# Keys and queries in two 40-row transfers, gates in the value rows, fillers ahead of the states, gate sums in two parts

## The chip, the cores and the metric

The program runs on 1 core of one Trainium2 chip. The metric is the device time of one execution in microseconds (us). Before the change three runs took 391.96 us in the median (391.62 to 394.35).

## What is computed

The reference is an mLSTM layer (4 sequences, 8 heads, 768 steps, head size 40) whose rows go through a mixture of 16 experts (4 groups of 4, one expert for each of 3,072 rows):

```
for t in range(S):
    m_new = max(f_gate[t] + m, i_gate[t])
    f_stab, i_stab = exp(f_gate[t] + m - m_new), exp(i_gate[t] - m_new)
    C = f_stab * C + i_stab * outer(v[t], k[t]);  n = f_stab * n + i_stab * k[t]
    y[t] = sigmoid(o_gate[t]) * (C @ q[t]) / max(abs(n @ q[t]), 1)
x = y as 3072 rows of 320
g, e = best group, best expert in it (argmax of two softmaxes)
out = weight_g * weight_e * (relu(x @ w1[g, e]) @ w2[g, e])
```

## The kernel before, in words

The first 138 us or so are the attention, cut into 24 units: unit u is chunk c = u // 4 (128 steps) of sequence b = u % 4, all 8 heads. Then come the experts, with weights from HBM.

A unit's work is written by `unit(u)` (L780 to 831), and each engine takes its instructions in that written order. `loads(u + 3)` (L161) issues on SP's queue the keys and queries of three units ahead (`qk`, one transfer of 112 rows of 4 KB, of which rows 40 to 63 and 104 to 111 are zeros), then the rows of values and keys (`nt`, 128 rows). The output gates of a whole chunk come in one further transfer (`sig`, L153), and `gate_o` (L158) puts them through Tanh on ACT once a chunk. On PE `scores` (L179, tile sp) multiplies keys by queries; DVE masks the result (`masked`, tile pt); `state` (L196, tile Cp) adds the unit to the running states; `carried` (L213, from chunk 1 on) and `values` (L221, tile av) give the numerators and denominators; ACT copies the states to Cz (`state2`). The next unit finishes the rows of this one: `norm` and `rows` on DVE (den, xn; `rows` reads the gates), `rows2` on POOL (x), `turn` transposes x on PE (tile tp). `vscale(u + 1)` (L170) on POOL scales the next unit's values by their gate factors (tile vz, from nt) and stands ahead of `rows2(u - 1)` on that engine.

The gate factors come from `gate_sums(lo, hi)` (L837): two scans and some sums on DVE, transposes on PE, exponentials on ACT. It is a generator; `sum_on` takes its next step once a unit (L807). Chunk 0 is done ahead of unit 0, chunk 1 in units 0 to 2, chunks 2 to 5 in one piece of 512 columns in units 3 to 7; in unit 7 it ends with a test (over) that PE sums. `route` steps (router and slots of a row) are taken by `go_on`, as many in a unit as the tables MID and END say. `busy(n)` (L122) issues n matmuls of 512 columns whose result nobody reads: 11 at the start, 6 in unit 0 between `state` and `carried`.

At most eight transfers issued by SP and ACT are in flight: each waits for the one issued eight before it.

Of the kernel before, what the change touches and what calls it, by code (L numbers as in the profile page):

```python
# [7 lines left out]
F32 = mybir.dt.float32  # L8
# [3 lines left out]
AF = mybir.ActivationFunctionType  # L12
# [6 lines left out]
P = 128  # L19
# [15 lines left out]
NQK = 4  # L35
QR = 112
C_ID, C_UP, C_LT, C_TIE, C_E, C_P, C_CAP, C_FIRST, C_15E, C_BASE, C_IOTA, C_END = 0, 128, 256, 384, 388, 404, 405, 421, 437, 453, 469, 581
NV = 4
RANGE = 30.0
SEQ = 4 * D + 3  # L40

# [18 lines left out]


@with_exitstack
def lstm_moe(ctx: ExitStack, tc: tile.TileContext, gates, qkT, nat, og, wcat, w1, w2, cst, seq, out):
    nc = tc.nc
    enter = ctx.enter_context
    mm = nc.tensor.matmul
# [40 lines left out]

    ap_ = att_pool("att", 1)

    qkp = [ap_.tile([P, 2, 4, P], F32, name=f"qk{i}") for i in range(NQK)]  # L110
    vz = [ap_.tile([P, H, P], F32, name=f"vz{i}") for i in range(3)]
    Cz = ap_.tile([P, B * 4, P], F32, name="Cz")
    eb = ap_.tile([P, NCH, B * H], F32, name="eb")
# [31 lines left out]
    def load_qk(u):  # L145
        c, b = divmod(u, B)
        qk = qkp[u % NQK]
        nc.sync.dma_start(qk[0:QR], qkT[c, b])
        st_.setdefault(u, {})["qk"] = qk

    sigs = {}

    def load_o(c):  # L153
        t = wk.tile([P, B, DM], F32, name="sig")
        nc.sync.dma_start(t, og[:, c * B:(c + 1) * B, :])
        sigs[c] = t

    def gate_o(c):  # L158
        nc.scalar.activation(sigs[c], sigs[c], AF.Tanh, scale=0.5)

    def loads(u):  # L161
        c, b = divmod(u, B)
        if u > 1:
            load_qk(u)
        nt = natp.tile([P, 2 * DM], F32, name="nt")
        nc.sync.dma_start(nt, nat[c, b])
        st_[u]["nt"] = nt

# [68 lines left out]
    def rows(u):  # L237
        c, b = divmod(u, B)
        xn = st_[u]["xn"] = wk.tile([P, H, D], F32, name="xn")
        nc.vector.scalar_tensor_tensor(xn, sigs[c][:, b, :].rearrange("p (h d) -> p h d", d=D), 1.0, st_[u]["av"][:, :, 0:D],  # L240
                                       op0=ALU.add, op1=ALU.mult)

    def rows2(u):
# [522 lines left out]
    def run(stage, u):  # L766
        if 0 <= u < NU:
            stage(u)

    def do(tasks, n=99):  # L770
        while tasks and n:
            tasks.pop(0)()
            n -= 1
# [5 lines left out]

    def unit(u):  # L780
        run(loads, u + 3)
        if u == 6:
            first_tokens()
        if u % B == 1 and u // B + 1 < NCH:
            load_o(u // B + 1)
        run(scores, u)
        run(norm, u - 1)
        run(rows, u - 1)
        if u < NU - 2:
            run(vscale, u + 1)  # L790
        if u == NU - 3:
            run(vscale, u + 2)
        run(rows2, u - 1)
        run(lambda v: masked(v, 0), u)
        run(lambda v: masked(v, 1), u)
        do(lows)
        run(state, u)
        if u % B == 1 and 1 < u < EUNITS:
            logits_of(u - 5, u - 1)
        if u == EUNITS + 1:  # L800
            logits_of(EUNITS - 2, EUNITS)
        if u == NU - 1:
            logits_of(EUNITS, NU - 2)
        if u == 0:
            busy(6)
        if u < 8:
            sum_on(SUMS.get(u, 1))  # L807
        run(carried, u)
        run(turn, u - 1)
        do(backs)  # L810
        if u == 10:
            go_on(2)
            chores.insert(0, first_experts())
        if u == EUNITS + 3:
            chores.append(early_counts())
        go_on(MID.get(u, 0))
        if u == NU - 1:
            do(rt["turns"])
        run(values, u)
        run(state2, u)  # L820
        go_on(END.get(u, 0))
        if u == 3:
            first_entries()
        if u == 5:
            first_rows()
        if u % B == 3 and u // B + 1 < NCH:
            gate_o(u // B + 1)
        for _ in range(min(rt.get("old", 0), 1 if u < 16 else 2)):
            put_id()
        rt["old"] = len(ids)  # L830
# [5 lines left out]
    def gate_sums(lo, hi):  # L836
        fg, ig = G[:, 0, lo:hi], G[:, 1, lo:hi]  # L837
        q = nc.gpsimd if lo == 0 else nc.vector
        init = NEG if lo == 0 else M_[:, lo - 1:lo]
        nc.vector.tensor_tensor_scan(M_[:, lo:hi], fg, ig, init, op0=ALU.add, op1=ALU.max)  # L840
        l1 = max(lo, 1)
        q.tensor_tensor(Cg[:, lo:hi], ig, M_[:, lo:hi], op=ALU.subtract)
        yield
        nc.vector.tensor_tensor(Dl[:, l1:hi], G[:, 0, l1:hi], M_[:, l1 - 1:hi - 1], op=ALU.add)
        nc.vector.tensor_tensor(Dl[:, l1:hi], Dl[:, l1:hi], M_[:, l1:hi], op=ALU.subtract)
        yield
        nc.vector.tensor_tensor_scan(A_[:, lo:hi], Dl[:, lo:hi], low[:, lo:hi], 0.0 if lo == 0 else A_[:, lo - 1:lo],
                                     op0=ALU.add, op1=ALU.max)
        q.tensor_tensor(Cg[:, lo:hi], Cg[:, lo:hi], A_[:, lo:hi], op=ALU.subtract)
        yield  # L850
        cl, ch = lo // P, hi // P
        tp = ps_1.tile([P, 512], F32, name="tp", tag="tp")
        n = ch - cl
        for i in range(n):
            s = slice((cl + i) * P, (cl + i + 1) * P)
            nc.tensor.transpose(out=tp[:, 32 * i:32 * i + 32], in_=Cg[:, s], identity=ident[0:32, 0:32])
            nc.tensor.transpose(out=tp[:, 32 * (n + i):32 * (n + i) + 32], in_=A_[:, s], identity=ident[0:32, 0:32])
        nc.scalar.activation(eb[:, cl:ch, :].rearrange("p c h -> p (c h)"), tp[:, 0:32 * n], AF.Exp)
        fl = floor[:, cl:ch, :].rearrange("p c h -> p (c h)")
        nc.scalar.activation(fl, tp[:, 32 * n:64 * n], AF.Exp, scale=-1.0)  # L860
        nc.vector.tensor_scalar(fl, fl, 2.0, None, op0=ALU.mult)
        if hi == S:
            yield
            over = post.tile([P, 1], BF16, name="over")[0:B * H]
            nc.vector.tensor_scalar(over, A_[:, S - 1:S], -RANGE, None, op0=ALU.is_le)
            tp = ps_1.tile([P, 512], F32, name="tp", tag="tp")
            mm(tp[:, 0:1], ones_b[0:B * H], over, start=True, stop=True)
            nc.vector.tensor_scalar(wide, tp[:, 0:1], 1.0, None, op0=ALU.min)
# [8 lines left out]
    with tc.manual_schedule():  # L877
        nc.sync.dma_start(G[:, :, 0:P], gates[:, :, 0:P])
        nc.scalar.dma_start(cs[:, 0:C_LT], cst[:, 0:C_LT])
        nc.scalar.dma_start(G[:, :, P:], gates[:, :, P:])  # L880
        nc.scalar.dma_start(cs[:, C_LT:], cst[:, C_LT:])
        nc.vector.memset(ones_b, 1.0)
        nc.vector.memset(ones16, float(NE))
        nc.vector.memset(sep, 0.0)
        nc.scalar.activation(sep, sep, AF.Exp)
        busy(11)
        nc.vector.memset(low, -RANGE)
        nc.vector.memset(Dl[:, 0:1], 0.0)
        nc.vector.memset(ohsum[0], 0.0)
        for t in Cp:  # L890
            nc.vector.memset(t, 0.0)
        for t in vz:
            nc.gpsimd.memset(t, 0.0)
        nc.gpsimd.memset(Cz, 0.0)
        load_qk(0)
        loads(0)
        load_qk(1)
        loads(1)
        load_o(0)
        loads(2)  # L900
        sums.append(gate_sums(0, P))
        sum_on(9)
        vscale(0)
        gate_o(0)
        nc.vector.tensor_copy(keyb, cs[:, C_15E:C_15E + NE])
        nc.vector.tensor_copy(lt_b, cs[:, C_LT:C_LT + P])
        nc.vector.tensor_copy(base_b, cs[:, C_BASE:C_BASE + NE])
        nc.sync.dma_start(wc, wcat)
        sums.append(gate_sums(P, 2 * P))
        sums.append(gate_sums(2 * P, S))  # L910
        for u in range(0, 5):
            unit(u)
    pools["ws"] = [wsa]
# [269 lines left out]
def _lay(inputs):  # L1183
# [5 lines left out]

    def tr(a):  # L1190
        a = a.reshape(B, H // 2, 2, NCH, P, D).transpose(3, 0, 2, 5, 1, 4)
        a = np.concatenate([a, np.zeros_like(a[:, :, :, :64 - D])], axis=3)
        return a.reshape(NCH, B, P, H // 2, P)[:, :, 0:QR]

    qkT = c(np.stack([tr(k), tr(q)], axis=3))

    def rows(a):
        return a.reshape(B, H, NCH, P, D).transpose(2, 0, 3, 1, 4)

    nat = c(np.concatenate([rows(v).reshape(NCH, B, P, DM), rows(k).reshape(NCH, B, P, DM)], axis=-1))  # L1200
    og = c(rows(o).reshape(NCH * B, P, DM).transpose(1, 0, 2))
    wg, we = inputs['moe_w_group'], inputs['moe_w_expert']
    wcat = np.concatenate([wg, we.transpose(1, 0, 2).reshape(DM, NE)], axis=1)
    wcat = np.pad(wcat, ((0, 0), (0, 12)))
# [21 lines left out]

    one = np.ones((S, B * H, 1), v.dtype)
    seq = c(np.concatenate([steps(q), steps(k), steps(v), one, steps(o), steps(inputs['f_gate']), steps(inputs['i_gate'])], axis=-1))
    return {'gates': gates, 'qkT': qkT, 'nat': nat, 'og': og, 'wcat': wcat, 'w1': w1, 'w2': w2, 'cst': cst, 'seq': seq}


# [20 lines left out]
```

## Time and profile before

| | us |
|---|---|
| median of three runs | 391.96 |
| the profiled execution, its own time | 389.81 |
| its span, first to last instruction | 387.9 |
| PE busy | 368.6 (95%) |
| DVE / ACT / POOL busy | 242.6 / 176.9 / 141.1 |

The profile follows one execution. Its chain of waits goes back from the last instruction, at each step to what released it. PE's busy share is not its share at its peak, since PE also runs at a lower granted clock in places. A stage is read by the wait that ends last in it.

### The profile page before, as it was taken

The page shows a single profiled execution, that of the slowest core. Times are in us where ns is not written, and L with a number is a line of the kernel's source. Part 1 is how long each engine was busy: PE and PEld are TensorE (multiplying, and loading weights), DVE is VectorE, ACT ScalarE, POOL GpSimd, SP SyncE. Part 2 cuts the span into 40 slices and gives each one's busy share as a digit, 9 for nine tenths or more (in the row PEclk, how much of TensorE's full clock was granted, in tenths as well). Part 3 has the DMA queues.
Part 4 walks back from the last instruction along what each step waited for, and adds up shares of the span by engine and source line. Part 5 has one row for each costly group of instructions (what it writes and reads, how often), then busy time and mean ns, then how long its engine had stood idle before and what let it go on. Part 6 is the DMA issues. An engine that isn't in the chain of part 4 may idle for free.

```text
span 387.9 us, 8856 instructions
## 1 busy us (share of the span) xinstructions
PE 368.6 (95%) x3313; PEld 348.1 (90%) x3313; DVE 242.6 (63%) x629; ACT 176.9 (46%) x411; POOL 141.1 (36%) x201
## 2 busy tenths in 40 slices
PE   6999999999998998899999999999999999999993
PEld 2688889989887998889999999999999999999993
DVE  4378757768777678466797757675574824554510
ACT  2233343426342233456665647656466633554520
POOL 6245225544646224625224253413413323233110
PEclk9799999999999899969999999999999999999998
DMA  7998767699983900859149977659525487669500
GB/s 190 304 323 265 199 192 234 182 325 289 318 276 92 356 32 1 246 172 356 69 129 414 373 268 259 198 183 355 179 84 182 165 306 251 226 254 328 189 19 16
DMA packets 26996, 85.34 MB, mean 220 GB/s; under 512 B 8800, under 2 KB 12339, under 8 KB 23362
## 3 DMA queue, kind: packets, MB, share of 16 engines
q1 hardware_dynamic: 18562, 66.35, 51.1%
q0 software_dynamic: 4560, 13.16, 10.1%
q10 hardware_dynamic: 3824, 5.18, 4.0%
q8 instruction: 28, 0.46, 0.5%
q14 instruction: 22, 0.18, 0.2%
HBM read 75.85 MB, written 9.10 MB: 219 GB/s over the span
## 4 chain that ended last, share of the span: by engine, by line
PE 80%; DVE 6%; issue 6%; DMA 4%; POOL 1%; POOLq 1%; ACT 1%; SPq 0%; DVEq 0%
PE psh L701 14%; PE av L225 10%; PE psh L669 8%; PE po L724 7%; PE po L725 7%; PE po L723 7%; PE sp L185 6%; PE av L218 4%; DMA nt<-in_nat_dram 4%; PE po L729 2%; PE tpm L251 2%; PE po L728 2%; PE tp L251 2%; PE Cp L202 2%; DVE pt L190 1%
## 5 line engine op out<-in xcount | busy, mean ns | idle before, releaser
L532 POOL DMA_INDIRECT out_dram<-y,ix x32 | 38.2, 1193 | 72.4 <-ACT y L735 57.9
L723 PE MATMUL po<-w2h,hh 128*128 128x320 f32 (+3 forms) x200 | 63.6, 318 | 0.0
L724 PE MATMUL po<-w2l,hh 128*128 128x320 f32 (+3 forms) x200 | 62.4, 312 | 0.0
L725 PE MATMUL po<-w2h,hh 128*128 128x320 f32 (+3 forms) x200 | 62.3, 311 | 0.0
L528 POOL DMA_INDIRECT xg<-x_d,ix x32 | 32.9, 1029 | 74.0 <-DMA ix<-itab 44.5
L596 DVE TENSOR_TENSOR w2l<-w2s,w2h 128x640 fp32r<-128x640 f32 x64 | 50.4, 817 | 12.7 <-ACT w2h L594 11.5
L225 PE MATMUL av<-vz,pt 128*128 128x128 f32 x384 | 49.8, 285 | 0.2
L658 DVE SCALAR_TENSOR_TENSOR hh<-psh,hh 128x240 fp32r<-128x240 f32 (+6 forms) x108 | 36.3, 366 | 21.1 <-ACT hh L655 20.1
L225 PEld LDWEIGHTS av<-vz,pt 128*128 128x128 f32 x384 | 47.2, 199 | 1.6 <-PE busy L128 1.0
L655 ACT ACTIVATE hh<-psh 128x288 fp32r<-128x288 f32 (+8 forms) x68 | 30.1, 443 | 32.9 <-PE psh L701 16.4
L594 ACT CAST w2h<-w2s 128x640 fp32r<-128x640 f32 x64 | 43.2, 722 | 0.0
L669 PE MATMUL psh<-xhl,w1s 128*128 128x144 f32 (+3 forms) x336 | 41.3, 283 | 0.0
L669 PEld LDWEIGHTS psh<-xhl,w1s 128*128 128x128 f32 x336 | 40.9, 191 | 0.0
L701 PE MATMUL psh<-xhl,w1h 128*128 128x256 f32 (+5 forms) x224 | 37.4, 289 | 0.0
L723 PEld LDWEIGHTS po<-w2h,hh 128*128 128x128 f32 (+3 forms) x200 | 36.6, 183 | 0.0
L724 PEld LDWEIGHTS po<-w2l,hh 128*128 128x128 f32 (+3 forms) x200 | 36.5, 183 | 0.0
L725 PEld LDWEIGHTS po<-w2h,hh 128*128 128x128 f32 (+3 forms) x200 | 36.5, 182 | 0.0
L735 ACT ACTIVATE y<-po,ix 128x320 f32<-128x320 f32 (+3 forms) x24 | 12.7, 529 | 48.3 <-PE po L725 41.6
L190 DVE TENSOR_TENSOR pt<-sp,cs 128x512 f32<-128x512 f32 x48 | 30.9, 685 | 3.3 <-PE sp L185 2.4
L433 POOL DMA_INDIRECT itab<-ent,slot x24 | 24.0, 1002 | 21.7 <-DVE ent L380 17.1
L701 PEld LDWEIGHTS psh<-xhl,w1h 128*128 128x128 f32 x224 | 31.2, 189 | 0.7 <-issue 0.2
L245 POOL TENSOR_TENSOR x<-xn,den 128x320 f32<-128x320 f32 x20 | 14.4, 722 | 43.7 <-DVE xn L240 29.6
(193 smaller groups left out, 683.6 us busy)
## 6 DMA issues: line engine op xcount, KB each, us to landing
w1s<-in_w_dram SPq DMA_DIRECT2D x13, 1536.0 KB
w2s<-in_w_dram SPq DMA_DIRECT2D x13, 1280.0 KB
qk<-in_qkT_dram SPq DMA_DIRECT2D x24, 448.0 KB
nt<-in_nat_dram SPq DMA_DIRECT2D x24, 320.0 KB
x_d<-x ACTq DMA_DIRECT2D x24, 192.0 KB
sig<-in_og_dram SPq DMA_DIRECT2D x6, 640.0 KB
w1s<-in_w_dram SPq DMA_DIRECT2D x8, 384.0 KB
w2s<-in_w_dram SPq DMA_DIRECT2D x8, 320.0 KB
```

The lines of the kernel that those rows point to most:

```text
L190: nc.vector.tensor_tensor(pt, t["pm"][r], bc(cs[:, C_UP:C_UP + P].unsqueeze(1), (P, 4, P)), op=ALU.mult)
L225: mm(t["av"][:, j * D1:j * D1 + P], t["pm"][j % 2][:, j // 2, :], t["vz"][:, j, :], start=(c == 0 and j == 0), stop=(j == H - 1), skip_gro ...
L528: return nc.gpsimd.indirect_dma_start(out=o, out_offset=None, in_=src, in_offset=bass.IndirectOffsetOnAxis(ap=idx, axis=0))
L532: return nc.gpsimd.indirect_dma_start(out=out, out_offset=bass.IndirectOffsetOnAxis(ap=idx, axis=0), in_=y, in_offset=None, bounds_check=N ...
L594: nc.scalar.copy(a, src[:, s])
L596: lows.append(lambda: nc.vector.tensor_tensor(o[rows], src[rows, s], a[rows].bitcast(F32), op=ALU.subtract))
L658: nc.vector.scalar_tensor_tensor(hh[:, f:f + per, dst], src[:, :, t], 0.0, hr.bitcast(F32)[:, :, t], op0=ALU.max, op1=ALU.subtract)
L669: ins = mm(ps[:, g * W:(g + 1) * W], w1s[:, s], xhl[:, k, :], start=(k == 0), stop=(k == 2))
L701: ins = mm(ps[:, g * W:(g + 1) * W], w[:, s], x, start=(n == 0), stop=(n == len(todo) - 1))
L723: mm(po[0:m], hh[:, f, t], w2h[:, s], start=st0, stop=False)
L724: mm(po[0:m], hh[:, f, t], w2l[:, s], start=False, stop=False)
L725: ins = mm(po[0:m], hh[:, f, tl], w2h[:, s], start=False, stop=sp0)
```

## The change

- Each unit's qk comes as two transfers of 40 rows (two pieces of 2 KB a row) straight into rows 0 to 39 and 64 to 103. The 32 zero rows are no longer sent; instead the query half of the four qk tiles is zeroed once, two tiles by DVE at the very start, two by POOL.
- The output gates are the last third of `nt` (128 rows of 3.75 KB instead of 2.5 KB), and the sig transfer goes. Tanh runs once a unit on 320 columns, after `values` and ahead of the Cz copies. There are five nt buffers instead of four.
- Fillers: 12 at the start instead of 11, 3 ahead of the first scores, and 5 between scores and state of unit 0 instead of 6 between state and values.
- POOL zeroes vz[2] and Cz after the first gate sums instead of ahead of them.
- The gate sums of chunks 2 to 5 come as 2 to 3 (units 3 to 6) and 4 to 5 (units 7 to 10), and the test over is made in unit 11 and summed on PE in unit 12.

```diff
-NV = 4
+NV = 5
...
-        nc.sync.dma_start(qk[0:QR], qkT[c, b])
-        st_.setdefault(u, {})["qk"] = qk
...
+        for r in range(2):
+            nc.sync.dma_start(qk[64 * r:64 * r + D], qkT[c, b, r].rearrange("g p t -> p g t"))
+        st_.setdefault(u, {})["qk"] = qk.rearrange("p g (h t) -> p g h t", t=P)
...
+    def gate_o(u):
+        o = st_[u]["nt"][:, 2 * DM:3 * DM]
+        nc.scalar.activation(o, o, AF.Tanh, scale=0.5)
...
-        nt = natp.tile([P, 2 * DM], F32, name="nt")
+        nt = natp.tile([P, 3 * DM], F32, name="nt")
...
-        if u % B == 1 and u // B + 1 < NCH:
-            load_o(u // B + 1)
...
         do(lows)
+        if u == 0:
+            busy(5)
         run(state, u)
...
-        if u == 0:
-            busy(6)
-        if u < 8:
+        if u < 13:
             sum_on(SUMS.get(u, 1))
...
         run(values, u)
+        gate_o(u)
         run(state2, u)
...
-        if u % B == 3 and u // B + 1 < NCH:
-            gate_o(u // B + 1)
...
             nc.vector.tensor_scalar(over, A_[:, S - 1:S], -RANGE, None, op0=ALU.is_le)
+            yield
...
+        for i in range(2):
+            nc.vector.memset(qkp[i][:, 1], 0.0)
...
-        busy(11)
+        busy(12)
...
-        for t in vz:
+        for t in (vz[0], vz[1], qkp[2][:, 1], qkp[3][:, 1]):
             nc.gpsimd.memset(t, 0.0)
-        nc.gpsimd.memset(Cz, 0.0)
...
-        load_o(0)
         loads(2)
         sums.append(gate_sums(0, P))
         sum_on(9)
+        busy(3)
+        nc.gpsimd.memset(vz[2], 0.0)
+        nc.gpsimd.memset(Cz, 0.0)
         vscale(0)
-        gate_o(0)
...
-        sums.append(gate_sums(2 * P, S))
+        sums.append(gate_sums(2 * P, 4 * P))
+        sums.append(gate_sums(4 * P, S))
```

PE at the start, before; tp are the gate sums, sp the scores, Cp the state, av the values of unit 0, and the last row is unit 1:

```order
L857 MATMUL tp<-cs,w2s 128x32
L185 MATMUL sp<-qk_100 128x128 x8
L202 MATMUL Cp_122<-vz_104,nt 40x41 x8
L128 LDWEIGHTS ones_b
L128 MATMUL busy<-ones_b 128x512
...
L225 MATMUL av_235<-vz_104,pt 128x128 x8
L185 MATMUL sp<-qk_101 128x128 x8
```

And now:

```order
L849 MATMUL tp<-cs,w2s 128x32
L128 LDWEIGHTS ones_b
L128 MATMUL busy<-ones_b 128x512
...
L180 MATMUL sp<-qk_100 128x128 x8
...
L197 MATMUL Cp_122<-vz_104,nt 40x41 x8
L220 MATMUL av_244<-vz_104,pt 128x128 x8
L180 MATMUL sp<-qk_101 128x128 x8
```

Nothing stands between state and values any more; three fillers stand ahead of the scores, five between scores and state.

POOL at the end of unit 3 and in units 4 and 5, before (the two vz are those of units 5 and 6, the two x those of units 3 and 4):

```order
L412 IOTA ent_74 128x2
L174 TENSOR_TENSOR vz_106<-nt,eb 128x8x40
L174 TENSOR_TENSOR vz_104<-nt,eb 128x8x40
L245 TENSOR_TENSOR x<-xn,den 128x320 x2
L418 MEMSET w1s 128x256
```

And now:

```order
L407 IOTA ent_74 128x2
L169 TENSOR_TENSOR vz_106<-nt,eb 128x8x40
L240 TENSOR_TENSOR x<-xn,den 128x320
L169 TENSOR_TENSOR vz_104<-nt,eb 128x8x40
L240 TENSOR_TENSOR x<-xn,den 128x320
```

The x of unit 3 no longer stands behind the vz of unit 6, which needs the nt of unit 6.

DVE in unit 7 behind the two masks, before:

```order
L190 TENSOR_TENSOR pt<-sp,cs 128x512 x2
L865 TENSOR_SCALAR over<-w2s 32x1
L868 TENSOR_SCALAR wide<-tp 128x1
L369 TENSOR_REDUCE sm<-ex 128x20
L371 TENSOR_SCALAR sm<-sm 128x20
```

And now:

```order
L185 TENSOR_TENSOR pt<-sp,cs 128x512 x2
L832 SCALAR_TENSOR_TENSOR w1s<-w1s 32x256
L834 TENSOR_TENSOR w1s<-w1s 32x256
L364 TENSOR_REDUCE sm<-ex 128x20
L366 TENSOR_SCALAR sm<-sm 128x20
```

The test over and its reader have left the unit; a scan and a subtraction of 256 columns have come.

## Rows read from the trace of the kernel before

**Rows 1.** The page's chain that ended last: shares of the span by engine

```profile
PE 80%; DVE 6%; issue 6%; DMA 4%; POOL 1%; POOLq 1%; ACT 1%; SPq 0%; DVEq 0%
```

**Rows 2.** Timeline of PE: start us, length us, instruction [idle before <-what ended it]

```profile
7.63 1.16 PE L185 MATMUL sp<-qk 40*128 40x128 f32 x16 [0.89 <-DMA qk<-in_qkT_dram]
10.04 0.78 PE L202 MATMUL Cp<-vz,nt 128*40 128x41 f32 x16 [1.25 <-POOL vz L174]
10.75 2.74 PE L128 MATMUL busy<-ones_b 128*128 128x512 bf16 x6
13.55 2.97 PE L225 MATMUL av<-vz,pt 128*128 128x128 f32 x16
16.45 1.16 PE L185 MATMUL sp<-qk 40*128 40x128 f32 x16
18.75 2.06 PE L225 MATMUL av<-vz,pt 128*128 128x128 f32 x16
20.75 1.16 PE L185 MATMUL sp<-qk 40*128 40x128 f32 x16
...
32.58 0.55 PE L251 MATMUL tp<-cs,x 128*128 128x128 f32 x3 [0.32 <-POOL x L245]
...
41.13 0.19 PE L328 MATMUL lg<-oh,lt_b 128*128 128x64 bf16 x1 [0.59 <-DVE oh L323]
...
49.31 0.17 PE L867 MATMUL tp<-over,ones_b 32*128 32x1 bf16 x1 [0.99 <-DVE over L865]
```

**Rows 3.** Timeline of POOL, units 0 to 2 and 4, columns as in Rows 2

```profile
9.27 0.72 POOL L174 TENSOR_TENSOR vz<-nt,eb 128x320 f32<-128x320 f32 x1 [2.89 <-DMA nt<-in_nat_dram]
...
16.39 0.72 POOL L174 TENSOR_TENSOR vz<-nt,eb 128x320 f32<-128x320 f32 x1 [4.07 <-DMA nt<-in_nat_dram]
17.59 0.72 POOL L245 TENSOR_TENSOR x<-xn,den 128x320 f32<-128x320 f32 x1 [0.48 <-DVE xn L240]
...
31.12 0.72 POOL L174 TENSOR_TENSOR vz<-nt,eb 128x320 f32<-128x320 f32 x1 [0.87 <-DMA nt<-in_nat_dram]
```

**Rows 4.** Busy time by stretch: length, engines' busy us, PEclk, DMA share, GB/s

```profile
5.75:8.84 3.09, 1.47 (x18) 1.17 (x18) 0.58 (x5) 0.50 (x3) 0.55 (x2) 0.97 1.06 285
8.84:15.25 6.41, 5.15 (x30) 3.06 (x31) 1.94 (x4) 1.67 (x4) 1.44 (x2) 0.50 1.04 309
...
122.00:124.00 2.00, 0.69 (x4) 0.49 (x5) 1.97 (x5) 0.38 (x2) 1.72 (x3) 1.00 0.02 1
124.00:128.00 4.00, 3.89 (x20) 3.48 (x22) 2.60 (x13) 0.35 (x1) 1.64 (x2) 0.59 0.82 238
```

**Rows 5.** The same for ten microseconds in the middle of the attention

```profile
80.00:90.00 10.00, 10.00 (x129) 9.19 (x125) 5.85 (x23) 4.16 (x13) 4.28 (x7) 1.00 1.04 318
```

**Rows 6.** The page's transfers by line: count, size of one

```profile
qk<-in_qkT_dram SPq DMA_DIRECT2D x24, 448.0 KB
nt<-in_nat_dram SPq DMA_DIRECT2D x24, 320.0 KB
...
sig<-in_og_dram SPq DMA_DIRECT2D x6, 640.0 KB
```

**Rows 7.** Chain of waits in order of time: start us, length us, what

```profile
22.42 8.57 DMA nt<-in_nat_dram
...
37.32 1.19 DVE w2s L847
38.53 1.03 DVE w1s L849
...
73.05 1.09 PE sp L185 x16
...
77.78 1.09 PE sp L185 x16
```

**Rows 8.** Groups by shape, first 60 us: busy us, mean ns | idle before

```profile
L159 ACT ACTIVATE sig<-sig 128x1280 f32<-128x1280 f32 x3 | 3.8, 1271 | 6.3 <-DMA sig<-in_og_dram 6.3
...
L891 DVE MEMSET Cp<- 128x512 f32 x2 | 1.0, 485 | 0.2
```

More of the change, by code (lines that the diff above doesn't have):

```diff
@@ L62, in lstm_moe @@
 @with_exitstack
-def lstm_moe(ctx: ExitStack, tc: tile.TileContext, gates, qkT, nat, og, wcat, w1, w2, cst, seq, out):
+def lstm_moe(ctx: ExitStack, tc: tile.TileContext, gates, qkT, nat, wcat, w1, w2, cst, seq, out):
     nc = tc.nc
@@ L108, in lstm_moe @@
     ap_ = att_pool("att", 1)
-    qkp = [ap_.tile([P, 2, 4, P], F32, name=f"qk{i}") for i in range(NQK)]
+    qkp = [ap_.tile([P, 2, 4 * P], F32, name=f"qk{i}") for i in range(NQK)]
     vz = [ap_.tile([P, H, P], F32, name=f"vz{i}") for i in range(3)]
@@ L147, in load_qk @@
         qk = qkp[u % NQK]
-        nc.sync.dma_start(qk[0:QR], qkT[c, b])
-        st_.setdefault(u, {})["qk"] = qk
[L151 to L159, printed above, removed]
+        for r in range(2):
[4 more added lines that the diff above has]
+        nc.scalar.activation(o, o, AF.Tanh, scale=0.5)
     def loads(u):
@@ L239, in rows @@
         xn = st_[u]["xn"] = wk.tile([P, H, D], F32, name="xn")
-        nc.vector.scalar_tensor_tensor(xn, sigs[c][:, b, :].rearrange("p (h d) -> p h d", d=D), 1.0, st_[u]["av"][:, :, 0:D],
+        nc.vector.scalar_tensor_tensor(xn, st_[u]["nt"][:, 2 * DM:3 * DM].rearrange("p (h d) -> p h d", d=D), 1.0, st_[u]["av"][:, :, 0:D],
                                        op0=ALU.add, op1=ALU.mult)
@@ L1191, in tr @@
         a = a.reshape(B, H // 2, 2, NCH, P, D).transpose(3, 0, 2, 5, 1, 4)
-        a = np.concatenate([a, np.zeros_like(a[:, :, :, :64 - D])], axis=3)
-        return a.reshape(NCH, B, P, H // 2, P)[:, :, 0:QR]
+        return a.reshape(NCH, B, 2, D, H // 2 * P)
     qkT = c(np.stack([tr(k), tr(q)], axis=3))
@@ L1198, in rows @@
         return a.reshape(B, H, NCH, P, D).transpose(2, 0, 3, 1, 4)
-    nat = c(np.concatenate([rows(v).reshape(NCH, B, P, DM), rows(k).reshape(NCH, B, P, DM)], axis=-1))
-    og = c(rows(o).reshape(NCH * B, P, DM).transpose(1, 0, 2))
+    nat = c(np.concatenate([rows(a).reshape(NCH, B, P, DM) for a in (v, k, o)], axis=-1))
     wg, we = inputs['moe_w_group'], inputs['moe_w_expert']
@@ L1228, in _lay @@
     seq = c(np.concatenate([steps(q), steps(k), steps(v), one, steps(o), steps(inputs['f_gate']), steps(inputs['i_gate'])], axis=-1))
-    return {'gates': gates, 'qkT': qkT, 'nat': nat, 'og': og, 'wcat': wcat, 'w1': w1, 'w2': w2, 'cst': cst, 'seq': seq}
+    return {'gates': gates, 'qkT': qkT, 'nat': nat, 'wcat': wcat, 'w1': w1, 'w2': w2, 'cst': cst, 'seq': seq}
 def kernel(**inputs):
```

## The prediction, made before the changed kernel was run

> **What bounds the kernel now.** I read the chain of waits first. PE carries 80% of it and transfers 4% [rows 1], so a microsecond counts only where it moves PE. In the middle of the attention one unit's scores start 4.73 us after the last unit's [rows 7] and PE is busy for all of a 10 us stretch [rows 5]: there PE alone sets the pace. Next I read PE's timeline for the places where it waits. The first 20 us are the slow part: unit 1's scores start only at 16.45 and unit 2's at 20.75 [rows 2]. Unit 0's values start at 13.55, although its state was there at 10.82; what stands between is 2.74 us of fillers [rows 2]. POOL's timeline shows the second limit: vz of unit 2 stood idle 4.07 us for its nt, started at 16.39, and x of unit 0 stands behind it, at 17.59 [rows 3]. The transfer engines were full all that time, share 1.04 at 309 GB/s [rows 4]. Later there are three short waits: 0.32 us for x of unit 3, 0.59 us for the router in unit 5, 0.99 us for the test over in unit 7 [rows 2].
>
> **Part 1, the start.** Without fillers behind the state, values of unit 0 can begin at 10.04 + 0.78 = 10.8. At unit 1's duration of 2.06 us they end near 12.9, so unit 1's scores come 3.5 us earlier than at 16.45 [rows 2]. That lead is not kept: unit 1 cannot turn unit 0's rows before x of unit 0, and x stands on POOL behind vz of unit 2, so nt of unit 2 decides. From vz to x is 0.72 us [rows 3], and from x to unit 2's scores 20.75 - 17.59 = 3.16 us [rows 2, 3]. Before, x also waited 0.48 us for xn [rows 3]; now xn is early, so even with nt landing when it does today 0.48 us is won.
>
> When does nt of unit 2 land? Ahead of its end the queue had three qk, three nt and one sig: 3 x 768 + 640 = 2,944 KB [rows 6]. Now it has 3 x (320 + 480) = 2,400 KB. At 309 GB/s the missing 544 KB are 1.8 us [rows 4]: the upper bound, a gain of 1.8 + 0.5 = 2.3 us. It holds if the sixteen transfer engines share a 40-row transfer evenly. All large loads so far have 112 or 128 rows, multiples of sixteen; 40 rows are not, and no row shows how they are dealt. If the busiest engine gets 3 of 40 rows of 4 KB, it carries 24 KB of keys and queries and 30 KB of nt a unit, 162 KB in three units, against 2,944 / 16 = 184 KB now: 22 KB less, 1.1 us at 309 / 16 = 19.3 KB/us. If it gets more, nt lands no earlier, or up to 1 us later (each unit's nt itself grows by 160 KB, 10 KB an engine, 0.5 us): the lower bound, a loss of about 0.5 us. I take 3 rows, the least a whole-row split allows: 1.1 + 0.5 = 1.6 us.
>
> The price is the clock. Unit 1's scores and state are done near 14.5 and PE then waits for x until about 16.5. After stretches in which PE was busy for 1.47 of 3.09 us, or 0.69 of 2.00, the granted clock was 0.50 in the next 6.41 us and 0.59 in 4 us [rows 4], the lower of its two levels, 1.2 GHz. Fillers bridge unit 0 now; none bridge unit 1. The bounds are nothing, if the clock stays, and 1.6 us, what the second of these stretches lost: 4 x (1 - 0.59). I take 0.9 us, the difference of unit 0's values at the lower clock and unit 1's at the higher, 2.97 - 2.06 [rows 2]. The start is then worth 1.6 - 0.9 = 0.7 us.
>
> The other moves at the start cost nothing. DVE's two memsets (2 x 0.485 us [rows 8]) delay the first scan by 1 us, but POOL's share of those sums no longer stands behind the memset of Cz, and the scores wait for qk until 7.63 anyway [rows 2]. POOL's vz[2] and Cz are zeroed while nt of unit 0 is under way (2.89 us of idling [rows 3]). If nt came earlier than that, the memsets would be late next. The first qk waits for one 0.485 us memset, behind SP's issue of the gates.
>
> **Part 2, x of unit 3.** On POOL it stood behind vz of unit 6, which waited until 31.12 for an nt that took 8.57 us [rows 3, 7]. It now stands ahead of it, and PE's 0.32 us [rows 2] go.
>
> **Part 3, gate sums.** In unit 5 DVE's scan of 512 columns and its subtraction, 1.19 + 1.03 us [rows 7], stand ahead of the router for which PE waits 0.59 us. With 256 columns each is shorter; if both halve, 1.1 us go, so all of the 0.59 goes. In unit 7 the 0.99 us for over go [rows 2]: over is made a unit ahead of its matmul. Against it stand about 1.1 us more of DVE work in each of units 7, 8 and 9, in units of 4.73 us, and four of the eight transposes move from unit 6 to unit 10. In unit 9 the new scan stands between the masks and the router. If that cover is gone, up to 0.6 us come back. I count none.
>
> **Part 4, Tanh.** Six of 1.27 us become 24 on a quarter of the columns, so at least 0.32 us each, and with a fixed share perhaps 0.5 [rows 8]. They stand ahead of the Cz copies, which are read four units later, and run beside `values`; the next unit's `rows` comes after `values`. Nothing, either way.
>
> **Sum.** 0.7 + 0.32 + 0.59 + 0.99 = 2.6 us. The profiled execution, 389.81 us with a span of 387.9, would come to 387.2. It was 2.15 us faster than the median of the runs, 391.96, and the forecast is for the median: **389.4 us**. What is won ahead of unit 8 shifts all that follows, since transfers, router and experts start relative to the units.
>
> **Rivals.**
> - **Everything is kept, 20%.** Forty rows are shared evenly and PE's clock stays up. The start is worth 2.3 us, the sum 4.2, the time 387.8. For it speaks that 14% fewer bytes go through full engines [rows 4, 6]; against it the idle time in unit 1.
> - **Ten engines carry the keys, 25%.** If a 40-row transfer is dealt over ten engines, four rows each, the busiest carry 320 / 10 + 480 / 16 = 62 KB a unit, against 928 / 16 = 58 KB now. Three units are 186 KB against 184: nt of unit 2 lands as late as before. The start wins 0.5 us and, with PE idle for some 3 us in unit 1, pays the clock's whole 1.6. With the other 1.9 us the sum is 0.8, the time 391.2. The Trainium skill says so ("DMA: Bandwidth & Descriptors", section "Why a DMA increments its semaphore by 16 and not by 1"): the engines used are the largest number up to 16 that divides the slowest dimension, as 100 partitions give 10. By that rule the time would be 391.2 rather than 389.4, and no run here shows it yet.
> - **The middle falls behind, 10%, slower.** From 80 us on the engines are full at 318 GB/s (share 1.04) while the first expert's weights load [rows 5]. With ten busy engines each unit takes 4 KB more on them, 0.2 us at 19.9 KB/us. Worse, SP has three loads a unit instead of 2.25, and only eight transfers may be in flight: with one weight load and one store a unit that is 8 / 5 = 1.6 units, 7.6 us, where landing took 8.57 [rows 7]. Ten such units lose 10 us of lead; the loads are issued three units, 14.2 us, ahead, so 14.2 - 8.57 = 5.6 us are spare. From the point where these are used up, PE waits for nt: some 4.4 us, less the 0.8 of the rival above, 395.6 us. Against it: today's chain has no such wait.
> - The remaining 45% are my forecast.
>
> **Range and chances.** About 1%, 3.9 us, is what a measurement of this kernel tells from no change. Faster by more needs nearly all of the first rival (below 388.0): 20% with the better end of the forecast. Slower by more (above 395.9) is half of the third: 6%. Within 1%: 74%. The range runs from 386.9, the first rival with both bounds of the small terms, to 393.0, the second rival with nt a microsecond late and the unit 9 cover gone.
>
> **What would show it.** Right: no fillers between Cp and av of unit 0, unit 1's scores near 13, vz of unit 2 near 15.3, unit 2's scores near 19 to 20, a stretch at half clock there; PE's waits for over and for the router in units 5 and 7 gone, none new in units 9 and 10. Wrong: vz of unit 2 at 16.4 or later (second rival), a granted clock of 1.00 throughout (first), or PE or POOL waiting for nt beyond 60 us (third).

## The result, and the profile after

The changed kernel took 388.5 us in the median of ten runs (385.58 to 391.75), the kernel before 392.15 in ten runs beside them: ratio 0.9889, 95% interval 0.9851 to 0.9926. A second series gave 388.55 us (twelve runs) against 391.38 (29 runs), ratio 0.9954, interval 0.9919 to 0.9988. The ratios leave out executions more than 1.5% above the shortest of their kernel, so they can differ from the ratio of the two medians. It is faster, by 2.8 to 3.7 us in the medians and 1.8 to 4.4 us by the ratios; forecast were 389.4 us and 2.6 us. The stages behind that sum came out otherwise than forecast.

The first profiled execution of the changed kernel was the longest of its ten, 391.75 us. Unless another is named, the rows below are of one near the median, 388.46 us, span 386.8. First PE's timeline of it, columns as in Rows 2:

```profile
7.71 1.16 PE L180 MATMUL sp<-qk 40*128 40x128 f32 x16
9.99 0.51 PE L197 MATMUL Cp<-vz,nt 128*40 128x41 f32 x16
10.52 2.33 PE L220 MATMUL av<-vz,pt 128*128 128x128 f32 x16
12.79 1.16 PE L180 MATMUL sp<-qk 40*128 40x128 f32 x16
13.88 0.51 PE L197 MATMUL Cp<-vz,nt 128*40 128x41 f32 x16
17.31 0.88 PE L246 MATMUL tp<-cs,x 128*128 128x128 f32 x3 [2.93 <-POOL x L240]
17.98 3.29 PE L220 MATMUL av<-vz,pt 128*128 128x128 f32 x16
21.20 1.16 PE L180 MATMUL sp<-qk 40*128 40x128 f32 x16
25.74 1.16 PE L180 MATMUL sp<-qk 40*128 40x128 f32 x16
...
32.56 0.49 PE L246 MATMUL tp<-cs,x 128*128 128x128 f32 x3
34.77 1.16 PE L180 MATMUL sp<-qk 40*128 40x128 f32 x16
...
40.37 0.19 PE L323 MATMUL lg<-oh,lt_b 128*128 128x64 bf16 x1
...
72.83 0.17 PE L860 MATMUL tp<-over,ones_b 32*128 32x1 bf16 x1
```

Against [rows 2]: unit 1's scores come 3.66 us earlier, at 12.79, but unit 2's, at 21.20, are 0.45 us later than at 20.75. Between them PE waits 2.93 us for x of unit 0. The waits for x of unit 3, for the router in unit 5 and for over are gone (32.56, 40.37 and 72.83 have no bracket). POOL's timeline shows why x is late:

```profile
12.40 0.72 POOL L169 TENSOR_TENSOR vz<-nt,eb 128x320 f32<-128x320 f32 x1 [2.66 <-DMA nt<-in_nat_dram]
15.74 0.72 POOL L169 TENSOR_TENSOR vz<-nt,eb 128x320 f32<-128x320 f32 x1 [2.61 <-DMA nt<-in_nat_dram]
16.42 0.84 POOL L240 TENSOR_TENSOR x<-xn,den 128x320 f32<-128x320 f32 x1
```

vz of unit 2 starts at 15.74, 0.65 us earlier than in [rows 3], and x of unit 0 stands behind it. Busy time by stretch, columns as in Rows 4:

```profile
14.00:15.00 1.00, 0.39 (x16) 0.26 (x14) 1.00 (x2) 0.00 (x0) 0.00 (x0) 1.00 0.74 271
15.00:16.00 1.00, 0.00 (x0) 0.00 (x0) 0.93 (x4) 0.00 (x0) 0.26 (x1) 1.00 0.70 220
...
16.00:18.00 2.00, 0.69 (x4) 0.69 (x5) 1.36 (x2) 0.24 (x1) 1.26 (x2) 0.84 0.89 247
18.00:20.00 2.00, 2.00 (x11) 2.00 (x11) 0.00 (x0) 1.53 (x5) 0.00 (x0) 0.50 0.86 311
20.00:22.00 2.00, 2.00 (x22) 1.88 (x23) 0.62 (x4) 0.00 (x0) 0.72 (x1) 0.81 0.84 266
```

While POOL waits for nt the transfer engines are busy for only 0.70 to 0.74 of the time (the number ahead of the last in a row), against 1.04 in [rows 4]. Behind the wait the granted clock falls to 0.50, the lower of its two levels. In the 391.75 us execution PE waited 3.52 us at that place and the clock then stayed at 0.50 until 30 us:

```profile
14.00:15.00 1.00, 0.00 (x0) 0.00 (x0) 1.00 (x3) 0.00 (x0) 0.00 (x0) 1.00 0.64 207
...
18.00:22.00 4.00, 4.00 (x20) 3.77 (x21) 0.14 (x1) 1.53 (x5) 0.72 (x1) 0.50 0.80 262
22.00:26.00 4.00, 3.53 (x37) 3.13 (x38) 2.24 (x7) 0.42 (x3) 1.47 (x2) 0.50 0.52 146
26.00:30.00 4.00, 4.00 (x22) 3.78 (x22) 0.22 (x2) 1.53 (x5) 0.00 (x1) 0.50 0.61 206
```

The page's transfers by line, beside [rows 6]:

```profile
nt<-in_nat_dram SPq DMA_DIRECT2D x24, 480.0 KB
qk<-in_qkT_dram SPq DMA_DIRECT2D x48, 160.0 KB
```

### The profile page after: what moved, and what is told of

The parts are those of the page before. It is cut to its first block, busy times and chain, and to the rows that moved or that the text cites. A ratio compares the mean times of both kernels' runs of the same rounds, so it can differ in the third digit from the quotient of the medians.

```text
span 390.1 us, 8956 instructions
## 1 busy us (share of the span) xinstructions
PE 371.0 (95%) x3316; PEld 350.4 (90%) x3316; DVE 246.7 (63%) x638; ACT 179.3 (46%) x431; POOL 146.9 (38%) x203
## 4 chain that ended last, share of the span: by engine, by line
PE 41%; issue 7%; DMA 6%; DVE 3%; POOL 1%; POOLq 1%; SPq 1%; ACT 0%
PE psh L696 9%; PE psh L664 8%; PE po L719 5%; PE po L720 5%; PE po L718 5%; DMA ix<-itab 4%; PE po L724 2%; DMA xg<-x_d,ix 2%; PE tpm L246 2%; PE po L723 2%; DVE w2l L591 1%; PE psh L675 1%; PE psh L678 1%; POOL xg L523 1%; POOLq L740 1%
## 5 line engine op out<-in xcount | busy, mean ns | idle before, releaser
L523 POOL DMA_INDIRECT xg<-x_d,ix x32 | 36.9, 1154 | 72.8 <-DMA ix<-itab 47.2
L220 PE MATMUL av<-vz,pt 128*128 128x128 f32 x384 | 51.3, 289 | 0.3
L220 PEld LDWEIGHTS av<-vz,pt 128*128 128x128 f32 x384 | 48.3, 204 | 1.3 <-DVE pt L185 0.8
```

Source lines behind the costliest of these rows:

```text
L220: mm(t["av"][:, j * D1:j * D1 + P], t["pm"][j % 2][:, j // 2, :], t["vz"][:, j, :], start=(c == 0 and j == 0), stop=(j == H - 1), skip_gro ...
L523: return nc.gpsimd.indirect_dma_start(out=o, out_offset=None, in_=src, in_offset=bass.IndirectOffsetOnAxis(ap=idx, axis=0))
```

## The experiments

Each variant was timed in five rounds beside the kernel before (a ratio below 1 is faster than before) and profiled. Starts of a unit's scores, from PE's timelines, in us; the row "from unit 13" is the span less unit 13's start:

| | before | before, second | changed | sums in one | fillers | x of 0 first | x of 0 to 2 first | x of 0 to 4 first | same as x of 0 to 2, 112 rows |
|---|---|---|---|---|---|---|---|---|---|
| execution | 389.81 | 391.73 | 388.46 | 389.38 | 387.89 | 389.48 | 384.14 | 382.79 | 391.51 |
| unit 1 | 16.45 | 15.20 | 12.79 | 12.94 | 12.94 | 12.97 | 12.30 | 12.89 | 12.79 |
| unit 3 | 25.28 | 24.72 | 25.74 | 25.02 | 23.81 | 26.33 | 21.13 | 21.72 | 21.63 |
| unit 5 | 34.84 | 37.98 | 34.77 | 34.04 | 32.84 | 35.36 | 31.13 | 30.75 | 38.52 |
| unit 13 | 77.71 | 80.67 | 76.25 | 76.94 | 74.37 | 76.86 | 72.61 | 72.21 | 79.98 |
| span | 387.9 | 389.8 | 386.8 | 387.6 | 386.2 | 387.8 | 382.4 | 381.1 | 389.9 |
| from unit 13 | 310.2 | 309.1 | 310.6 | 310.7 | 311.8 | 310.9 | 309.8 | 308.9 | 309.9 |

**The gate sums in one piece.**

```diff
             nc.vector.tensor_scalar(over, A_[:, S - 1:S], -RANGE, None, op0=ALU.is_le)
-            yield
...
-        sums.append(gate_sums(2 * P, 4 * P))
-        sums.append(gate_sums(4 * P, S))
+        sums.append(gate_sums(2 * P, S))
```

> The changed kernel with the gate sums of chunks 2 to 5 in one piece, and with over where it was before: part 3 alone undone. Theory (the middle gives the gain): the waits in unit 5 (0.59 us for the router) and in unit 7 (0.99 us for over) come back, 1.6 to 2.3 us slower than the changed kernel, 390 to 391. Rival (the start gives the gain and the middle is covered): within 0.7 us of the changed kernel, 388 to 389.

Measured: 390.38 us, 1.8 above the changed kernel; ratio 0.998 (0.9942 to 1.0018). That interval overlaps the changed kernel's, and it is the trace that separates the two. PE's timeline has both waits again:

```profile
40.33 0.19 PE L323 MATMUL lg<-oh,lt_b 128*128 128x64 bf16 x1 [0.58 <-DVE oh L318]
...
48.51 0.17 PE L859 MATMUL tp<-over,ones_b 32*128 32x1 bf16 x1 [0.99 <-DVE over L857]
```

From unit 5 to unit 13 it takes 42.90 us, the changed kernel 41.48, and every other variant with split sums 41.46 to 41.53: 1.4 us that do not depend on the start, as the theory said.

**Fillers in unit 1.**

```diff
         run(carried, u)
+        if u == 1:
+            busy(12)
         run(turn, u - 1)
```

> The changed kernel with twelve fillers on PE in unit 1, between unit 0's carried rest and its turn, where PE stood idle for 3.5 us (13.99 to 17.51) and the granted clock then was 0.50 until 30 us. Theory: the start loses its lead in two steps, nt of unit 2 lands no earlier and the idle time takes the clock. With the fillers the idle time is filled, the clock stays above 0.95 from 10 to 40 us, vz of unit 2 still starts near 16, unit 2's scores stay near 21 and unit 3's come near 25.5 instead of 29.57; 3 to 4.5 us less than the profiled execution of the changed kernel (391.75), and near the lowest of its times: 385 to 386.5. Rival (the idle time is not what takes the clock): the stretch at 0.50 is still there and the time stays at 388 to 390. Second rival (the clock there is hidden, since the transfers set the pace anyway): the clock stays up, unit 4's scores still come at 33 to 34.

Measured: 389.76 us, ratio 0.999 (0.9954 to 1.0027), no gain on the changed kernel. PE's timeline, and a stretch of the profiled execution (387.89, the shortest of its twelve):

```profile
14.47 2.76 PE L128 MATMUL busy<-ones_b 128*128 128x512 bf16 x12
17.07 0.49 PE L246 MATMUL tp<-cs,x 128*128 128x128 f32 x3
17.39 1.95 PE L220 MATMUL av<-vz,pt 128*128 128x128 f32 x16
```

```profile
10.00:40.00 30.00, 28.88 (x375) 25.17 (x376) 21.00 (x56) 10.29 (x37) 11.71 (x38) 1.00 0.79 250
```

The clock stays at 1.00 and unit 1's values take 1.95 us instead of 3.29, so the idle stretch is what takes the clock. But the time missed the theory's 385 to 386.5 and lies where the rival had it. Fillers do not make x come earlier; of the 1.93 us by which unit 3's scores are ahead of the changed kernel's (23.81 against 25.74), 0.80 come from an nt that landed earlier in this execution (x at 15.62 instead of 16.42). It gave back 1.2 us behind unit 13; whether that is the rule for this variant stays open.

**x of unit 0 ahead of vz of unit 2.**

```diff
+        if u == 1:
+            run(rows2, u - 1)
         if u < NU - 2:
             run(vscale, u + 1)
...
-        run(rows2, u - 1)
+        if u != 1:
+            run(rows2, u - 1)
```

> The changed kernel with one exchange on POOL: in unit 1 the second half of unit 0's rows, with x, comes ahead of vz of unit 2. Theory (x of unit 0 stands behind vz of unit 2, which waits for nt): x comes at about 14.0 instead of 16.74, PE turns unit 0's rows near 14.5 instead of 17.51, the idle time in unit 1 falls below 1 us; the next wait is for unit 2's state (vz) or unit 2's scores, which need keys only, and come near 18 instead of 21.75. The clock then stays near 1.0 until 30 us; 384.5 to 387. Rival (transfers set the pace of the start, not the order on POOL): PE waits as long a little later, in unit 2 for vz at 16 or in unit 3 for its keys, the clock falls there, and the time stays at 387.5 to 389.5.

Measured: 387.76 us (383.61 to 389.94), ratio 0.9888 (0.9845 to 0.9931). PE's timeline of an execution of 389.48 us:

```profile
14.90 0.55 PE L246 MATMUL tp<-cs,x 128*128 128x128 f32 x3 [0.30 <-POOL x L240]
...
22.48 0.55 PE L246 MATMUL tp<-cs,x 128*128 128x128 f32 x3 [3.38 <-POOL x L240]
```

The wait in unit 1 fell to 0.30 us, and the same wait came a unit later: x of unit 1 stands behind vz of unit 3, which waits for its own nt until 21.03. The theory's place is right, its forecast of the next wait (state or scores of unit 2) was not, and the median lies in the rival's range. The profiled execution is the third longest of the twelve.

**x of units 0 to 2 first**, the same edit with `1 <= u <= 3`.

> The changed kernel with x of units 0, 1 and 2 ahead of the next unit's vz on POOL (the earlier run did so for x of unit 0 alone; there x of unit 1 then stood behind vz of unit 3, which started at 21.03, and PE waited 3.38 us for it). Theory (the place of x on POOL behind a vz that waits for nt is what makes PE idle): no wait of PE for x above 1 us before 30 us, unit 3's scores at 21.5 to 23.5 instead of 29.57, no stretch at half clock before 40 us; 1.5 to 3 us faster than the run with one exchange (387.8), 384.5 to 386.5. Rival (the transfers set the pace, PE only waits elsewhere): PE waits for vz ahead of Cp of units 2 and 3, or for keys of unit 3, by as much, unit 4's scores come at 30 or later as in the run with one exchange (30.63), and the time is 387 to 389.

Measured: 384.52 us (383.90 to 385.39, six runs), ratio 0.9846 (0.9797 to 0.9895). PE's and POOL's timelines, and the stretch:

```profile
14.24 0.55 PE L246 MATMUL tp<-cs,x 128*128 128x128 f32 x3 [0.33 <-POOL x L240]
...
28.86 0.55 PE L246 MATMUL tp<-cs,x 128*128 128x128 f32 x3 [0.75 <-POOL x L240]
```

```profile
13.46 0.72 POOL L240 TENSOR_TENSOR x<-xn,den 128x320 f32<-128x320 f32 x1
15.87 0.83 POOL L169 TENSOR_TENSOR vz<-nt,eb 128x320 f32<-128x320 f32 x1 [1.68 <-DMA nt<-in_nat_dram]
...
30.77 0.72 POOL L169 TENSOR_TENSOR vz<-nt,eb 128x320 f32<-128x320 f32 x1 [1.96 <-DMA nt<-in_nat_dram]
```

```profile
10.00:40.00 30.00, 28.05 (x382) 25.57 (x382) 21.47 (x58) 10.79 (x40) 13.42 (x39) 1.00 0.84 263
```

vz of unit 2 starts no earlier than in the changed kernel (15.87), yet unit 3's scores come 4.6 us earlier, the clock keeps 1.00, and the lead holds to the end. It was POOL's order, not the transfer's landing, that cost the start.

**x of units 0 to 4 first** (`1 <= u <= 5`).

> As the run with x of units 0 to 2 ahead of the next unit's vz, now units 0 to 4. There PE still waited 0.75 us in unit 4 for x of unit 3, which stood behind vz of unit 5. Theory (the place of x on POOL): that wait goes too, 0 to 1 us faster than that run's 384.5: 383.5 to 384.5, and its narrow spread (383.90 to 385.39) stays. Rival: vz of units 5 and 6 now come late for Cp, and the time is 384.5 to 385.5.

Measured: 383.96 us (382.79 to 384.67), ratio 0.9841 (0.9791 to 0.9892): the fastest kernel here, though half a microsecond from the last is within what these runs tell. The 0.75 us wait is gone:

```profile
28.54 0.49 PE L246 MATMUL tp<-cs,x 128*128 128x128 f32 x3
```

**The changed kernel once more.**

> The changed kernel itself once more, beside the others on one chip. The four variants run so far had the same or a longer median than its 388.5 and an earlier start in their profiles. Theory (the profiled execution, with 13 us at half clock, was an unlucky one, and most executions are like that of the variant without split sums: 4 to 5 us at half clock, unit 3's scores near 25): a median of 388 to 389, and unit 3's scores at 24.5 to 26.5. Rival (the start of this kernel always costs 13 us at half clock): unit 3's scores near 29.5 again, with a like median.

Measured: 388.55 us (387.64 to 391.22). The profile shown first is this run's: about 10 of the 13 us at half clock were that one execution's, and the first theory holds.

**48 rows a transfer.**

```diff
-            nc.sync.dma_start(qk[64 * r:64 * r + D], qkT[c, b, r].rearrange("g p t -> p g t"))
+            nc.sync.dma_start(qk[64 * r:64 * r + 48], qkT[c, b, r].rearrange("g p t -> p g t"))
```

> The changed kernel with 48 rows in each key and query transfer instead of 40 (eight rows of zeros are added): 384 KB a unit instead of 320. Theory (a 40-row transfer goes over ten of the sixteen engines): with 48 = 3 x 16 rows all sixteen carry it, the DMA share between 14 and 16 us rises from 0.65 to about 1.0, and in spite of the added bytes nt of unit 2 lands 1 to 1.5 us earlier, vz of unit 2 starts near 15 instead of 16.01, and PE idles 2 to 2.5 us in unit 1 instead of 3.5; about 1 us faster than the changed kernel, 386.5 to 388. Rival (the number of issues and the transfers in flight make nt late, not the engines): three issues a unit as before, so vz of unit 2 stays at 16 or comes later by the added bytes, 3 x 64 KB at 309 GB/s = 0.6 us, and the time is 388.5 to 389.5.

Measured: 390.12 us, ratio 0.9975 (0.9938 to 1.0013). Stretches and POOL's timeline:

```profile
14.00:16.00 2.00, 0.40 (x16) 0.28 (x16) 1.93 (x5) 0.00 (x0) 0.00 (x0) 1.00 1.05 283
16.00:18.00 2.00, 0.38 (x3) 0.39 (x4) 0.94 (x2) 0.24 (x1) 1.45 (x2) 0.97 1.05 278
```

```profile
16.11 0.72 POOL L169 TENSOR_TENSOR vz<-nt,eb 128x320 f32<-128x320 f32 x1 [2.45 <-DMA nt<-in_nat_dram]
```

Half the theory holds: with 48 rows the share rises to 1.05, so 40 rows do leave engines idle. The other half falls: nt lands no earlier. From 5 to 20 us the engines moved 262 GB/s here at a share of 1.06, and 265 GB/s in the changed kernel at 0.91; between executions of the variants with 40 rows this rate varies from 251 to 290.

**Keys and queries in one 112-row transfer**, gates still in nt.

```diff
-        for r in range(2):
-            nc.sync.dma_start(qk[64 * r:64 * r + D], qkT[c, b, r].rearrange("g p t -> p g t"))
+        nc.sync.dma_start(qk[0:QR], qkT[c, b])
```

> The changed kernel with keys and queries in one transfer of 112 rows as before (24 rows of them zeros), the gates still in the value rows: 928 KB a unit as before instead of 800. By bytes: the 128 KB more a unit are 384 KB ahead of nt of unit 2, 1.2 to 1.4 us at 270 to 309 GB/s, so vz of unit 2 near 17, and 1 us or more slower than the changed kernel, 389.5 to 390.5. By engines (the two 40-row transfers lose by going over ten engines what they save in bytes): vz of unit 2 within 0.5 us of the changed kernel's 15 to 16, and the same time, 388 to 389.

Measured: 389.76 us, ratio 0.9974 (0.9934 to 1.0013), vz of unit 2 at 15.69. The landing speaks for engines, the time for bytes. One landing cannot settle it: with the same loads vz of unit 2 started between 14.94 and 16.01 in four profiles whose start is alike up to there. This program also has x of unit 3 behind vz of unit 6 again, as shown further down, so the run undoes part 2 together with the loads.

**The moved fillers and memsets alone**, in the kernel before.

```diff
-        if u == 0:
-            busy(6)
...
+        if u == 0:
+            busy(5)
         run(state, u)
...
-        nc.gpsimd.memset(Cz, 0.0)
...
+        busy(3)
+        nc.gpsimd.memset(vz[2], 0.0)
+        nc.gpsimd.memset(Cz, 0.0)
```

> The kernel before with the moved fillers and memsets only: no fillers behind unit 0's state, five behind its masks, vz[2] and Cz zeroed while nt of unit 0 is under way. Theory (the start's lead is lost, since x of unit 0 stands behind vz of unit 2 and nt lands no earlier): unit 1's scores come near 13, unit 2's at 20 to 22, and the time is within 1 us of before, 391 to 392.5, or slower by the half clock. Rival (the start is the gain): 389 to 390.

Measured: 389.82 us (388.69 to 393.27), ratio 0.999 (0.9951 to 1.0028): the median lies in the rival's range, the ratio says no change. In its profile unit 1's scores come at 11.96, unit 2's at 20.62, and PE waits 1.66 us for x. The lead is lost in the same place with the loads of before.

**The same with x of units 0 to 2 first**, and **the changed kernel with 112 rows and x of units 0 to 2 first**.

> The kernel before with the moved fillers and memsets, and x of units 0 to 2 ahead of the next unit's vz; loads and gate sums as before. Theory (the moved fillers gain nothing only because x then stands behind vz): the start of the run with the exchange in the changed kernel comes back, unit 3's scores at 21 to 22.5; against that run 1.4 to 1.9 us are missing in units 5 and 7, so 386 to 387, and a spread below 3 us. Rival (the new loads are what lets the exchange pay): unit 3's scores at 24 or later, 388.5 to 390.

> The changed kernel with keys and queries in one 112-row transfer and x of units 0 to 2 ahead of the next unit's vz: the whole change and the exchange, without the two 40-row transfers. Theory (how the keys travel sets neither nt nor the time, since all sixteen engines at a share of 1.05 move 250 to 300 GB/s and ten move as much at 0.8): within 0.7 us of the same with 40 rows (384.5): 384 to 385.3. Rival (fewer bytes do help once PE no longer waits for x): 1 to 1.5 us slower, 385.5 to 386.5. Second rival (forty rows over ten engines cost): faster, below 384.

Measured: 391.39 us (385.80 to 393.71), ratio 0.9961 (0.9914 to 1.0007), and 390.64 us (388.23 to 393.50), ratio 1.002 (0.9979 to 1.0061). Both medians missed the theory by 4 to 7 us. The times of the first lie in two groups, six up to 390.65 and six from 392.14; the profiled execution, 392.97, is of the longer ones. In its start the rival was right: unit 3's scores come at 24.07. ACT's, DVE's and POOL's timelines in unit 1:

```profile
14.63 1.27 ACT L159 ACTIVATE sig<-sig 128x1280 f32<-128x1280 f32 x1 [8.00 <-DMA sig<-in_og_dram]
15.93 0.49 DVE L240 SCALAR_TENSOR_TENSOR xn<-sig,av 128x320 f32<-128x320 f32 x1 [2.21 <-ACT sig L159]
16.50 0.72 POOL L245 TENSOR_TENSOR x<-xn,den 128x320 f32<-128x320 f32 x1 [3.52 <-DVE xn L240]
```

x of unit 0 is first on POOL here and comes late all the same, since xn waits for gates that still travel in the sig transfer. In the changed kernel with the same exchange x starts at 13.46. The Tanh of the sig transfer ends at 15.90 here and at 14.23 to 14.84 in the three other profiles that have it, so in unit 1 the exchange pays in full only together with the gates in nt.

Up to unit 4 the second variant starts like its 40-row twin; then PE's and POOL's timelines and the stretches show

```profile
34.93 0.90 PE L245 MATMUL tp<-cs,x 128*128 128x128 f32 x3 [6.33 <-POOL x L239]
38.52 1.16 PE L179 MATMUL sp<-qk 40*128 40x128 f32 x16
```

```profile
16.73 0.72 POOL L168 TENSOR_TENSOR vz<-nt,eb 128x320 f32<-128x320 f32 x1 [2.06 <-DMA nt<-in_nat_dram]
...
33.48 0.72 POOL L168 TENSOR_TENSOR vz<-nt,eb 128x320 f32<-128x320 f32 x1 [3.48 <-DMA nt<-in_nat_dram]
34.16 0.72 POOL L239 TENSOR_TENSOR x<-xn,den 128x320 f32<-128x320 f32 x1
```

```profile
32.00:34.00 2.00, 0.00 (x0) 0.00 (x0) 0.00 (x0) 0.00 (x0) 0.52 (x1) 0.50 1.03 246
34.00:36.00 2.00, 1.07 (x5) 1.07 (x6) 0.00 (x0) 0.38 (x2) 0.88 (x2) 0.50 1.06 253
```

The program with 112 rows has vz of unit 6 ahead of x of unit 3 on POOL, as the kernel before has; with two 40-row transfers x comes first. The source has `rows2(3)` ahead of `vscale(6)` in all of them, so at this place the program's order is not the written one. These two variants thus kept the very order that part 2 of the change removes. In their profiled executions it cost 4.37 and 6.33 us of idling and the clock. It does not always cost that: the 112-row run without the exchange and the run of the moved fillers alone have the same order, vz of unit 6 waited there not at all or 0.28 us, and unit 4 took 4.74 and 4.73 us.

The later landings fit the bytes: against the 40-row twin, vz of unit 2 starts 0.86 us later and vz of unit 6, where both wait for nt, 2.71 us later (33.48 against 30.77; unit 1's scores are 0.49 apart), and 128 KB more a unit make 896 KB by then, 3.4 us at 270 GB/s. That is one execution against one. In the two variants of the kernel before with moved fillers, whose loads are the same and whose unit 1 starts 1.05 us apart, vz of unit 6 waited for nt until 30.72 and 33.97, so the bytes are not shown to be the cause. What the loads are worth when x comes first in all five units was not tried.

**The kernel before, a second profile.**

> The kernel before once more, for a second look at its stages. Its profiled execution took 389.81 us, 1.6 to 2.1 less than its medians (391.4 to 392.15), and between the two profiles the changed kernel's gain is 1.1 to 1.4 us where the medians give 2.8 to 3.65. If the missing 1.5 us lie in the start of its usual executions, unit 3's scores come at 26 to 27.5 instead of 25.28 in an execution of 391 us or more; if they lie behind the attention, unit 13's scores stay at 52.4 us behind unit 3's and at 77.7, and the rest takes 311.5 us or more instead of 310.2.

Measured: 391.73 us, span 389.8. It fits neither place that was expected. Unit 3's scores come at 24.72, earlier than in the first profile, and the rest from unit 13 takes 309.1 us. The time is lost in unit 4:

```profile
32.31 1.07 POOL L174 TENSOR_TENSOR vz<-nt,eb 128x320 f32<-128x320 f32 x1 [1.85 <-DMA nt<-in_nat_dram]
33.35 0.72 POOL L245 TENSOR_TENSOR x<-xn,den 128x320 f32<-128x320 f32 x1
```

```profile
34.12 0.90 PE L251 MATMUL tp<-cs,x 128*128 128x128 f32 x3 [2.41 <-POOL x L245]
37.98 1.16 PE L185 MATMUL sp<-qk 40*128 40x128 f32 x16
```

The wait that was 0.32 us in [rows 2] is 2.41 us here, with a granted clock of 0.53 from 34 to 36 us: unit 4 takes 8.96 us instead of 5.27 (4.74 in the changed kernel).

## Why the prediction held in its sum, step by step

What the changed execution of 388.46 us gains on the two executions of before, from the table:

| stage | forecast | on 389.81 | on 391.73 |
|---|---|---|---|
| start, to unit 3's scores | 0.7 | -0.46 | -1.02 |
| units 3 and 4 (x of unit 3) | 0.32 | 0.53 | 4.23 |
| units 5 to 12 (router, over) | 1.58 | 1.39 | 1.21 |
| from unit 13 | 0 | -0.36 | -1.42 |
| span | 2.6 | 1.1 | 3.0 |

- **The start failed in sign**, in two terms. Nt of unit 2 was to land 1.1 us earlier, and 0.5 us more was to come from xn: 1.6 us. x came 17.59 - 16.42 = 1.17 us earlier. The clock was priced at 0.9 us, as one unit's values; from x to unit 2's scores it took 21.20 - 16.42 = 4.78 us instead of 3.16, which is 1.62, the upper bound. 1.17 - 1.62 = -0.45. The clock was the second rival's term.
- **Three of forty rows on the busiest engine** was the wrong choice: a share of 0.64 in one execution and 0.70 to 0.74 in another, rising to 1.05 with 48 rows, fits ten of sixteen engines, 0.63, with a little other work. The packets in the traces say the same: in moments from 5 to 31 us when pieces of 2 KB (keys and queries) are in flight and none of nt is, there are most often 10 of them at once in the changed kernel and never more than 13, with 48 rows most often 16 and up to 21. The trace agrees with the rule of the Trainium skill ("DMA: Bandwidth & Descriptors", section "Why a DMA increments its semaphore by 16 and not by 1"), by which 40 rows go over ten engines and 48 over sixteen. The step behind it failed in forecast and rival alike: both set the landing by what the busiest engine carries. By that count 48 rows would bring 3 x (24 + 30) = 162 KB instead of 186, 1.2 us earlier at 19.3 KB/us; measured, in one execution, is 16.11, later than in the four profiles with 40 rows. What sets the landing instead stays open; bytes in all fit the 40-row and 112-row twins, but no run here separates them from the spread between executions.
- **Part 2 was right in mechanism and too small in size.** 0.32 us is what one profiled execution lost; another of the same kernel lost 2.41 us and the clock, and its unit 4 took 3.7 us more. The forecast took a price from one execution for a wait whose end is a transfer's landing. How often before runs the one way or the other, two profiles don't tell, and no run undid part 2 by itself.
- **Part 3 was right**, 1.58 forecast and 1.39 or 1.21 measured. The waits of 0.59 and 0.99 are gone. The parts ahead of the router fell to 0.73 + 0.77 us, not to half of [rows 7], and that was enough. Units 5 to 7 gain 2.1 us, and 0.7 come back, where "up to 0.6" was named and none counted: unit 9 takes 6.29 us instead of 6.16, unit 10 with its four transposes 5.09 instead of 4.74, unit 12 with the sum of over 4.95 instead of 4.73.
- **The rivals.** The third did not come: PE has no wait for nt in the middle. The first was wrong on the clock and on how forty rows are dealt. The second had the engines and the clock right, though nt came 0.65 us earlier than it said; its 391.2 us left out what part 2 may save in executions slower than the profiled one.

So it is in part luck that the sum was near the median: a start that was 1.2 to 1.7 us worse than forecast met an x of unit 3 that in usual executions may be worth several times its term. Only part 3 came out as it was worked out.

## What to carry to other kernels

An engine that takes its work in order and stands waiting for a transfer also holds what is queued behind it: ask what that is before asking how to make the transfer faster. Here moving one finished piece of work ahead of the waiting one, in three to five units, gave another 4 to 4.6 us, where fillers and fuller transfers gave none. That needs the piece to be finished by then: with the gates in a transfer of their own x of unit 0 was not. Read the price of a wait that ends with a transfer from more than one execution.

## What the runs showed of the hardware

- From 5 to 20 us transfer engines that were busy for 1.04 to 1.06 of the time moved 262 to 304 GB/s in seven executions, and at 0.85 to 0.92 of the time 251 to 290 GB/s in seven others: the busy share alone doesn't show a bound.
- After PE stood still for 2.93 to 3.5 us the clock was 0.50 for some 3.5 us in one execution and 13 us in another of the same program.
- The start of vz of unit 2, which waits for nt, varied by about a microsecond between executions with the same loads (14.94 to 16.01). The twelve runs of the changed kernel with x of units 0 to 2 or 0 to 4 first lie between 382.8 and 385.4 us; the 22 of the changed kernel itself spread from 385.6 to 391.8.
